# Moving SBUF buffers by multiples of 32 bytes under a stream of float32r matmuls: eight buffers 32 bytes apart in their rest by 256, all later large buffers at rest 224

## The chip, the cores and the metric

The kernel runs on one core of one Trainium2 chip. The metric is the device time of one execution in microseconds (us); lower is better. The time of the kernel before is the median of three runs.

Two words are used throughout. The **rest** of a buffer is the byte at which it begins in each SBUF partition, modulo 256. The **distance** of a matmul is the rest of its weight operand minus the rest of its moving operand, modulo 256.

## The reference, cut to what matters

```python
x = A_x                                   # (1, 2048, 512), float32
xn = _layernorm(x, axis=-1)
a = jnp.einsum("bsd,ed->bse", xn, dft_hid_re)
b = jnp.einsum("bsd,ed->bse", xn, dft_hid_im)
s = jnp.einsum("ts,bse->bte", dft_seq_re, a) - jnp.einsum("ts,bse->bte", dft_seq_im, b)
h = jnp.einsum("bsd,df->bsf", xn, w1) + b1   # w1: (512, 1792)
r = jnp.where(h > 0, h, 0)
g = jnp.einsum("bsf,fd->bsd", r * r, w2) + b2   # w2: (1792, 512)
return x + s * _silu(g)
```

## The kernel before

Every float32 operand is split into a high part in float32r and a low part (the rest after the high part is taken away), and each product is three matmuls: high by high, high by low, low by high (`PASSES`). Most products are also done by a scheme of seven block products in place of eight, whose block sums VectorE forms. A stage therefore has long runs of matmuls of 128 by 128 weights and 256 moving columns, with a new weight load before nearly each one. The order of the instructions on each engine is written out by hand (`manual_schedule`).

TensorE does, in this order:

- **The plain stage**, line 340, 384 matmuls of 512 columns: the sequence transform of the first two chunks. The weights are x's normalised operands, buffers `xc0` to `xc7`; the moving operands are the split transform tiles in `ga` and `gb`, in turn.
- **The seven-product transform**, line 325, 2016 matmuls: six more chunks of 256 rows, each over eight steps j. Weights are `xc{j}`, moving operands `ga` (j even) or `gb` (j odd). 42 matmuls to a step.
- **The hidden transform**, line 705, class `YUnit`, 672 matmuls, 84 to a unit: weights are `yg` in `xc2` to `xc7`, moving operands `wdp` in `wd0`, `wd1`, `xc0`, `xc1`.
- **The first layer**, line 705, class `HUnit`, 1176 matmuls, 42 to a unit: weights are w1's blocks p = 0 to 6 in `ga`, `gb`, `xc2`, `xc3`, `xc0`, `xc1`, `wd0`; moving operands are `xT` in `xc6` and `xc7`, or in `xc4` and `xc5` for every other chunk of 512 rows. A unit's last products (5, 4 and 3) are done after the next unit has begun.
- **The second layer**, line 811, 1176 matmuls, 42 to a step: weights are `g` in `xc6`, `xc7`, `xc4` by the step's number modulo 3 (the very last in `wd0`); moving operands are w2's blocks p = 0 to 6 in `wd1`, `ga`, `gb`, `xc2`, `xc3`, `xc0`, `xc1`.

Each such buffer is one tag of the one SBUF pool, and its tile is larger than 256 bytes by a whole multiple (14336 bytes for `xc`, `ga`, `gb`; up to 16384 for `wd0`, `wd1`). Within a tile all matmul operands begin at multiples of 512 bytes. So each operand has the rest of its buffer.

A tag gets its place when it is first asked for, in steps of 32 bytes, one behind the other, and keeps it. In the kernel before, the pool's first tile stands at byte 1152, and `b1s`, `b2s`, `eps`, `stats` and `stats_t` end at byte 3552, which is 13 x 256 + 224. The places that follow are:

| buffers, in order | rest by 256 |
|---|---|
| `xc0` to `xc7` (line 170) | 224 |
| `pq00`, three `u`, `pq01`, `pq10`, `pq11`, `wd1` | 224 |
| three `bn` of 64 bytes, three `sm` of 32 bytes (288 bytes) | 224, 32, 96, 160, 192, 224 |
| `ga`, `wd0`, `gb`, `e` | 0 |

The distances of the stages before are thus: line 340 and line 325, 224 throughout (weights at 224, moving operands at 0); the hidden transform, 0 for three of four matmuls and 224 for the one with `wd0`; the first layer, 32 for p = 0, 1, 6 and 0 for p = 2, 3, 4, 5; the second layer, 224 for p = 1, 2 and 0 for p = 0, 3, 4, 5, 6 (32 for the last step).

Of the kernel before, what the change touches and what calls it, by code (L numbers as in the profile page):

```python
# [8 lines left out]
F32 = mybir.dt.float32  # L9
F32R = mybir.dt.float32r  # L10
# [3 lines left out]
P = 128  # L14
S, D, F = 2048, 512, 1792
NS, ND, NF = S // P, D // P, F // P
NJ, NP = NS // 2, NF // 2
# [102 lines left out]
def fnet_gated_kernel(ctx, tc, x, xt, ct, wd, w1, w2, b1, b2, out):  # L120
# [9 lines left out]
    def split(*parts):  # L130
        split_hi(*parts)
        split_lo(*parts)
# [4 lines left out]
    pool = ctx.enter_context(tc.tile_pool(name="pool", bufs=1))  # L137
# [5 lines left out]
    eps = pool.tile([P, 1], F32, name="eps")  # L143
    stats = pool.tile([P, 2, 2, NJ], F32, name="stats")
    stats_t = pool.tile([P, 2 * NS], F32, name="stats_t")
    rows = dram.tile([2 * NS, P], F32, name="rows")
    Y = [dram.tile([TC, D], F32, name=f"y{t}") for t in range(NTC)]
    PQD = [dram.tile([P, 2, 4, 256], F32, name=f"pqd{c}") for c in range(NC)]
# [10 lines left out]
    def buf(tag, shape, name, dtype=F32):  # L159
        bufs = {"u": 3, "bn": 3, "sm": 3}.get(tag, 1)  # L160
        return pool.tile(shape, dtype, tag=tag, bufs=bufs, name=name)
# [4 lines left out]
    def halves(ap):  # L166
        return ap.rearrange("p (a b) -> p a b", a=2)


    XC = [buf(f"xc{j}", [P, 7, 2, 256], f"xc{j}", F32R) for j in range(NJ)]  # L170

    xr, xn32 = {}, {}

# [5 lines left out]

    def ln_stats(j, hs=slice(0, 2)):  # L180
        t = xr[j]
        sm = buf("bn", [P, 12], f"bn{j}_{hs.start}")
        for h in range(hs.start, hs.stop):
            bn = sm[:, 6 * h:6 * h + 6]
            nc.vector.bn_stats(bn, t[:, h])  # L185
            nc.vector.bn_aggr(stats[:, :, h, j], bn)

    root = {}

    def ln_root(j, hs=slice(0, 2)):  # L190
        n = hs.stop - hs.start
        t = root[j] = buf("sm", [P, 4], f"root{j}_{hs.start}")
        nc.scalar.activation(t[:, 0:n], stats[:, 1, hs, j], AF.Sqrt, bias=eps)

    def ln_rstd(j, hs=slice(0, 2)):
# [17 lines left out]
    def xc_parts(j, h):  # L213
        s = slice(2 * h, 2 * h + 2)
        return XC[j][:, s, HI, :], XC[j][:, s, LO, :], halves(xn32[j][:, h])

# [14 lines left out]
    def split_sums(j):  # L231
        s = xn32[j].rearrange("p h (b n) -> p (h b) n", b=2)
        split(XC[j][:, S2:S4 + 1, HI, :], XC[j][:, S2:S4 + 1, LO, :], s[:, 0:3])
        return 0.9

    def split_s1(j):
        split(XC[j][:, S1, HI, :], XC[j][:, S1, LO, :], s1[j // ND][:, j % ND])
        return 0.4
# [81 lines left out]
    def mm(ps, w, mv, first, last):  # L320

        ps = ps.rearrange("p (i d t) -> p d i t", i=2, d=2)
        for d in range(2):
            for a_, b_ in PASSES:
                nc.tensor.matmul(ps[:, d], w[:, a_, d * P:(d + 1) * P], halves(mv(b_)),  # L325
                                 start=first and d == 0 and (a_, b_) == (HI, HI),
                                 stop=last and (a_, b_) == (LO, HI), skip_group_check=True)
# [9 lines left out]
    def one_product(c, j, h, k, passes=PASSES):  # L337
        for a_, b_ in passes:
            w = XC[j][:, 2 * h + k // 2, a_, k % 2 * P:(k % 2 + 1) * P]
            nc.tensor.matmul(accs[c][k], w, part[c, j][:, b_, 2 * h:2 * h + 2],  # L340
# [97 lines left out]
    for count, zeros in zip(WARM, (idle[:, 0:256].bitcast(mybir.dt.bfloat16), idle[:, 256:768])):  # L438
# [3 lines left out]
        for _ in range(count):  # L442
            nc.tensor.matmul(warm, zeros[:, 0:P], zeros, start=True, stop=True)
    ln_stats(0)
    ln_root(0)
    split_hi(*plain_parts(0, 0, one))
    ln_rstd(0)
# [5 lines left out]
    for hs in (one, two):  # L453
        split_lo(*plain_parts(0, 0, hs))
    split_lo(*xc_parts(0, 0))
    ln_stats(1)
    g = plain_parts(0, 1)
    split_hi(*g)
    ln_root(1)
    split_lo(*xc_parts(0, 1))  # L460
    for h in range(2):
# [3 lines left out]
    for j in range(1, NJ):  # L465
        ln_rstd(j)
        for h in range(2):
            ln_xn(j, h)
            split_hi(*xc_parts(j, h))
        split_lo(*g)  # L470
        load_c(*order[j + 3])
        if j + 4 < NJ:
            load_x(j + 4)
        split_lo(*xc_parts(j, 0))
        if j + 1 < NJ:
            ln_stats(j + 1)
            ln_root(j + 1)
        split_lo(*xc_parts(j, 1))
        for h in range(2):
            products(0, j, h)  # L480
        g = plain_parts(*order[j + 1])
        split_hi(*g)
        if j == 2:
            nc.sync.dma_start(b1s, b1)
            nc.sync.dma_start(b2s, bcast(b2, D))
# [58 lines left out]
    for n, s in enumerate(steps):  # L544
        c, j = s
# [4 lines left out]
        for p in FIRST if j == 0 and c > PLAIN else ORDER:  # L550
# [4 lines left out]
            a, b = PRODUCTS[p]  # L555
            mm(ms[p], XC[j][:, a], lambda b_: g[:, b_, b], j == 0, j == NJ - 1)
        border = closing and j == 0
# [335 lines left out]
    for u in range(1, NC):  # L893
        n = 2 * u + 2
# [184 lines left out]
def _launch(arrays, out_shape):  # L1079
    import numpy as np  # L1080
    import concourse.bacc as bacc
    from concourse.bass_utils import run_bass_kernel_spmd

    nc = bacc.Bacc("TRN2", target_bir_lowering=False, num_devices=1, dynamic_dma_scratch_size=1024)
    feed, args = {}, []
    for name, v in arrays.items():
        v = np.ascontiguousarray(v)
        feed[f"in_{name}"] = v
        args.append(nc.dram_tensor(f"in_{name}", v.shape, mybir.dt.from_np(v.dtype), kind="ExternalInput").ap())
    args.append(nc.dram_tensor("out_0", out_shape, F32, kind="ExternalOutput").ap())  # L1090
    with tile.TileContext(nc, schedule_with_timeline_sim=True) as tc:
        fnet_gated_kernel(tc, *args)
    r = run_bass_kernel_spmd(nc, [feed], core_ids=[0])
    return r.results[0]["out_0"]
# [25 lines left out]
```

## Time and profile before

| what | value |
|---|---|
| median of three runs | 702.4 us (702.17 to 702.65) |
| the profiled execution | 701.75 us |
| its span, first to last instruction | 700.0 us |
| granted TensorE clock, mean | 0.998 |
| line 340, first and last start | 7.7 and 97.7 us |
| line 325 | 97.9 and 333.9 us |
| line 705, hidden transform | 334.0 and 417.0 us |
| line 705, first layer | 410.7 and 557.1 us |
| line 811 | 552.9 and 695.2 us |

The profiled execution is one run, 1.75 us longer than its span. In the views, PE is TensorE's matmuls, PEld its weight loads, DVE is VectorE, ACT is ScalarE. A matmul's record lasts longer than the time until the next one begins, because matmuls overlap in the engine; the time that counts is the **pace**, from one start to the next. From a row of the timeline, which joins equal instructions that follow each other, the pace is the row's length less one record (0.28 us for 256 columns), over the count less one.

### The profile page before, as it was taken

The numbers are of one execution on the slowest core, as the hardware profiler recorded it, in microseconds if no ns is written. First come the engines' busy times: TensorE is split into PE (matmuls) and PEld (weight loads), VectorE is DVE, ScalarE is ACT, GpSimd is POOL, SyncE is SP. The second block draws the span as 40 slices with busy tenths as digits, with TensorE's granted clock in tenths as the row PEclk, the third lists the DMA queues.
The fourth block names the chain that finished last, engine by engine and source line by source line (L and its number), as shares of the span: only waits on it lengthen the run. The fifth ranks groups of instructions, "written<-read, shape, count | busy, mean of one in ns | idle before, by whom it ended". The sixth has DMA issues, their size and how long they took to land.

```text
span 700.0 us, 13144 instructions
## 1 busy us (share of the span) xinstructions
PE 693.0 (99%) x5440; PEld 670.1 (96%) x5440; DVE 605.6 (87%) x849; ACT 357.9 (51%) x475; POOL 6.4 (1%) x9
## 2 busy tenths in 40 slices
PE   8999999999999999999999999999999999999997
PEld 5778889999999999999999999999999999999997
DVE  7999769999999898788899788899748689989896
ACT  4436544435343343435455358777778764444451
POOL 0000000000000000000000000000000000101000
PEclk9999999999999999999999999999999999999999
DMA  8535756768486754367488457587426956767745
GB/s 298 198 104 197 257 202 219 257 204 290 158 294 211 259 210 166 121 239 274 151 287 280 151 185 287 195 322 266 154 118 197 388 168 188 194 197 195 227 155 157
DMA packets 51723, 150.82 MB, mean 215 GB/s; under 512 B 4944, under 2 KB 19536, under 8 KB 50256
## 3 DMA queue, kind: packets, MB, share of 16 engines
q1 hardware_dynamic: 44096, 129.80, 54.9%
q10 hardware_dynamic: 6208, 18.88, 6.8%
q0 software_dynamic: 1360, 1.31, 1.5%
q8 instruction: 42, 0.69, 0.4%
q14 instruction: 17, 0.14, 0.1%
HBM read 101.98 MB, written 47.99 MB: 214 GB/s over the span
## 4 chain that ended last, share of the span: by engine, by line
PE 94%; DVE 3%; DMA 1%; ACT 1%; issue 1%; SPq 0%; DVEq 0%; ACTq 0%
PE m L325 33%; PE m_o L811 15%; PE r_B L705 13%; PE r_A L705 8%; PE pq_b L340 8%; PE r_C L705 4%; PE r_D L705 4%; PE m_last L811 4%; PE pq_ba L340 2%; PE pq_bc L340 1%; PE pq_bb L340 1%; DMA rows<-rows 1%; DVE yg L128 0%; DMA x<-in_x 0%; DVE bn L185 0%
## 5 line engine op out<-in xcount | busy, mean ns | idle before, releaser
L325 PEld LDWEIGHTS m<-g,xc 128*128 128x128 f32 x2016 | 235.7, 188 | 0.6 <-DVE g L128 0.2
L325 PE MATMUL m<-g,xc 128*128 128x256 f32 x2016 | 236.2, 280 | 0.0
L125 ACT ACTIVATE g<-u 128x1792 fp32r<-128x1792 f32 (+3 forms) x70 | 100.1, 1431 | 143.2 <-PE m L325 47.7
L128 DVE TENSOR_TENSOR g<-u,g 128x1792 fp32r<-128x1792 f32 (+3 forms) x70 | 117.5, 1679 | 23.3 <-ACT g L125 23.1
L811 PE MATMUL m_o<-w,g 128*128 128x256 f32 x882 | 105.7, 282 | 0.0
L811 PEld LDWEIGHTS m_o<-w,g 128*128 128x128 f32 x882 | 105.5, 191 | 0.0
L125 ACT ACTIVATE g<-hr 128x1792 fp32r<-128x1792 f32 (+2 forms) x31 | 47.9, 1556 | 47.2 <-PE m_o L811 25.2
L705 PE MATMUL r_B<-xT,w 128*128 128x256 f32 x504 | 69.4, 282 | 0.0
L340 PE MATMUL pq_b<-g,xc 128*128 128x512 f32 x240 | 66.7, 397 | 1.1 <-ACT xc L125 1.0
L705 PEld LDWEIGHTS r_B<-xT,w 128*128 128x128 f32 x504 | 64.1, 190 | 0.0
L128 DVE TENSOR_TENSOR g<-hr,g 128x1792 fp32r<-128x1792 f32 (+2 forms) x31 | 56.7, 1837 | 7.1 <-ACT g L125 7.1
L340 PEld LDWEIGHTS pq_b<-g,xc 128*128 128x128 f32 x240 | 43.8, 188 | 13.9 <-ACT xc L125 3.1
L705 PE MATMUL r_A<-xT,w 128*128 128x256 f32 x336 | 44.7, 282 | 0.0
L705 PEld LDWEIGHTS r_A<-xT,w 128*128 128x128 f32 x336 | 42.1, 190 | 0.0
L705 PE MATMUL r_B<-wdp,yg 128*128 128x256 f32 x288 | 37.5, 283 | 0.2 <-DVE y L715 0.2
L705 PEld LDWEIGHTS r_B<-wdp,yg 128*128 128x128 f32 x288 | 35.6, 190 | 0.6 <-DVE y L715 0.4
L811 PE MATMUL m_last<-w,g 128*128 128x256 f32 x294 | 35.1, 282 | 0.0
L811 PEld LDWEIGHTS m_last<-w,g 128*128 128x128 f32 x294 | 35.1, 190 | 0.0
L257 DVE TENSOR_TENSOR u<-u 128x512 f32<-128x512 f32 x48 | 32.8, 684 | 1.7 <-DMA u<-in_ct 1.7
L128 DVE TENSOR_TENSOR yg<-yraw,yg 128x1792 fp32r<-128x1792 f32 x13 | 26.2, 2021 | 5.4 <-ACT yg L125 5.4
L306 DVE TENSOR_TENSOR c<-m,c 128x512 f32<-128x512 f32 x42 | 27.2, 684 | 1.7 <-PE m L325 1.0
L125 ACT ACTIVATE yg<-yraw 128x1792 fp32r<-128x1792 f32 x13 | 22.1, 1699 | 7.2 <-DVE yraw L266 5.5
(180 smaller groups left out, 862.7 us busy)
## 6 DMA issues: line engine op xcount, KB each, us to landing
u<-in_ct SPq DMA_DIRECT2D x63, 512.0 KB, 3.7
hd<-h ACTq DMA_DIRECT2D x28, 512.0 KB, 4.8
hr<-hd SPq DMA_DIRECT2D x28, 512.0 KB, 3.9
wdp<-wdd SPq DMA_DIRECT2D x8, 896.0 KB, 7.2
yraw<-pqd SPq DMA_DIRECT2D x13, 512.0 KB, 5.0
pqd<-c SPq DMA_DIRECT2D x6, 1024.0 KB, 4.4
w<-w1d SPq DMA_DIRECT2D x6, 896.0 KB, 8.7
y<-y ACTq DMA_DIRECT2D x8, 512.0 KB, 4.1
```

Source lines behind the costliest of these rows:

```text
L125: nc.scalar.activation(hi, src, AF.Copy)
L128: nc.vector.tensor_tensor(lo, src, hi.bitcast(F32), op=ALU.subtract)
L257: nc.vector.tensor_tensor(t[:, 0:2], r[:, 0:1].to_broadcast([P, 2, 256]), r[:, 1:3], op=ALU.add)
L306: nc.vector.tensor_tensor(part_(to), m, part_(frm), op=op)
L325: nc.tensor.matmul(ps[:, d], w[:, a_, d * P:(d + 1) * P], halves(mv(b_)), start=first and d == 0 and (a_, b_) == (HI, HI), stop=last and ( ...
L340: nc.tensor.matmul(accs[c][k], w, part[c, j][:, b_, 2 * h:2 * h + 2], start=j == 0 and h == 0 and (a_, b_) == (HI, HI), stop=j == NJ - 1 a ...
L705: nc.tensor.matmul(self.region(REGION[k]), w, mv, start=i == 0 and k in (1, 7), stop=i == len(ops) - 1, skip_group_check=True)
L811: nc.tensor.matmul(m[:, i * 256:(i + 1) * 256], ready[n][:, a_, H_SLOT[a], i * P:(i + 1) * P], W2[p][:, b_, b], start=p == 0 and i == 0 an ...
```

## The change

The tags `bn` and `sm` are asked for ahead of the `xc` buffers, and after each of `xc0` to `xc6` a tile of 32 bytes that nothing uses is asked for. No other statement changes; the first `bn` and `sm` tiles are taken from the small dictionary in place of a new request.

```diff
     rows = dram.tile([2 * NS, P], F32, name="rows")
+    small = {tag: pool.tile([P, n], F32, tag=tag, bufs=3, name=f"{tag}0_0") for tag, n in (("bn", 12), ("sm", 4))}
...
-    XC = [buf(f"xc{j}", [P, 7, 2, 256], f"xc{j}", F32R) for j in range(NJ)]
+    XC = []
+    for j in range(NJ):
+        XC.append(buf(f"xc{j}", [P, 7, 2, 256], f"xc{j}", F32R))
+        if j < NJ - 1:
+            pool.tile([P, 8], F32, name=f"gap{j}")
...
-        sm = buf("bn", [P, 12], f"bn{j}_{hs.start}")
+        sm = small.pop("bn", None) or buf("bn", [P, 12], f"bn{j}_{hs.start}")
...
-        t = root[j] = buf("sm", [P, 4], f"root{j}_{hs.start}")
+        t = root[j] = small.pop("sm", None) or buf("sm", [P, 4], f"root{j}_{hs.start}")
```

By the same rule of placing, `xc0` begins at 3552 + 288 = 3840 = 15 x 256, rest 0; each next `xc` is 14336 + 32 bytes further, so `xc{j}` has rest 32j; everything behind `xc7` (rest 224) has rest 224, `ga`, `gb`, `wd0`, `wd1` and `e` included. Counted over all matmuls in program order (each one's moving operand against the weights that are loaded while it runs), the distances become:

| stage, matmuls | distance 0 | 32 | 64 | 96 | 128 | 160 | 192 | 224 |
|---|---|---|---|---|---|---|---|---|
| line 340, before | 0 | 0 | 0 | 0 | 0 | 0 | 0 | 384 |
| line 340, after | 48 | 48 | 48 | 48 | 48 | 48 | 48 | 48 |
| line 325, before | 0 | 0 | 0 | 0 | 0 | 0 | 0 | 2016 |
| line 325, after | 252 | 251 | 252 | 253 | 252 | 252 | 252 | 252 |
| other three, before | 1973 | 546 | 0 | 0 | 0 | 0 | 0 | 504 |
| other three, after | 308 | 237 | 291 | 525 | 469 | 569 | 256 | 368 |

On line 325 the distance after is 32(j + 1) modulo 256, so each of the eight steps j has one of its own.

## The prediction

> **What bounds the kernel now.** I read the page first: busy time, then the chain that ended last, then its groups.
>
> ```profile
> span 700.0 us, 13144 instructions
> PE 693.0 (99%) x5440; PEld 670.1 (96%) x5440; DVE 605.6 (87%) x849; ACT 357.9 (51%) x475; POOL 6.4 (1%) x9
> ...
> PE 94%; DVE 3%; DMA 1%; ACT 1%; issue 1%; SPq 0%; DVEq 0%; ACTq 0%
> ...
> L325 PE MATMUL m<-g,xc 128*128 128x256 f32 x2016 | 236.2, 280 | 0.0
> ```
>
> TensorE is busy for 99% of the span and makes 94% of the chain; the largest group, line 325, has no idle time ahead of it. So the time is the number of matmuls times their pace, and the question is whether an operand's address alters the pace. Next I read the timeline of PE alone, which joins runs of equal matmuls, in stretches whose buffers I know from the order of the steps. First the second layer (line 811): steps with w2 in `xc3`, `xc0`, `xc1`, `wd1`, then the two with w2 in `ga` and `gb`. The weights are in `xc` buffers, rest 224, in both.
>
> ```profile
> 574.77 20.56 PE L811 MATMUL m_o<-w,g 128*128 128x256 f32 x170
> ```
>
> ```profile
> 594.93 10.30 PE L811 MATMUL m_o<-w,g 128*128 128x256 f32 x86
> ```
>
> The pace is (20.56 - 0.28)/169 = 120.0 ns where both operands rest at 224, distance 0, and (10.30 - 0.28)/85 = 117.9 ns where the moving operand rests at 0, distance 224. Line 325, also at distance 224, and line 340, the same but with 512 columns:
>
> ```profile
> 112.61 24.90 PE L325 MATMUL m<-g,xc 128*128 128x256 f32 x212
> ```
>
> ```profile
> 53.10 2.26 PE L340 MATMUL pq_b<-g,xc 128*128 128x512 f32 x9
> ...
> 58.70 2.26 PE L340 MATMUL pq_b<-g,xc 128*128 128x512 f32 x9
> ```
>
> Line 325 paces (24.90 - 0.28)/211 = 116.7 ns. Line 340 does 24 matmuls from 53.10 to 58.70, 233.3 ns each, twice 116.7. With 512 columns a weight load has twice the time to finish, so I take 116.7 ns as what streaming 256 columns costs when the weight load doesn't hinder: a floor, and line 325 stands on it already. The first layer (line 705), from one `r_D` to the one a unit later, 42 matmuls: first with w1 at rest 224 (distance 0), then with w1 in `wd0` and `ga` at rest 0 (distance 32).
>
> ```profile
> 429.96 0.88 PE L705 MATMUL r_D<-xT,w 128*128 128x256 f32 x6
> ...
> 435.00 0.88 PE L705 MATMUL r_D<-xT,w 128*128 128x256 f32 x6
> ```
>
> ```profile
> 450.03 0.87 PE L705 MATMUL r_D<-xT,w 128*128 128x256 f32 x6
> ...
> 455.00 0.87 PE L705 MATMUL r_D<-xT,w 128*128 128x256 f32 x6
> ```
>
> That is 5.04/42 = 120.0 ns and 4.97/42 = 118.3 ns. The hidden transform has three distances of 0 to one of 224, 84 matmuls to a unit:
>
> ```profile
> 354.79 1.60 PE L705 MATMUL r_D<-wdp,yg 128*128 128x256 f32 x12
> ...
> 364.82 1.60 PE L705 MATMUL r_D<-wdp,yg 128*128 128x256 f32 x12
> ```
>
> 10.03/84 = 119.4 ns, where (3 x 120.0 + 117.9)/4 gives 119.5: one price for each distance carries over between stages. The weight loads show the same split. Below is the view of one line's weight loads (least, median and greatest duration in ns), at distance 0, at distance 224, and in the opening matmuls of line 443, whose weights and moving operand are the same zeros at rest 224.
>
> ```profile
> L811 PEld LDWEIGHTS m_o<-w,g x43: 191/192/193, 574.9 to 579.9; 128*128 128x128 f32 x43
> ```
>
> ```profile
> L811 PEld LDWEIGHTS m_o<-w,g x42: 187/188/192, 595.1 to 599.9; 128*128 128x128 f32 x42
> ```
>
> ```profile
> L443 PEld LDWEIGHTS warm<-idle x8: 187/188/338, 4.2 to 6.1; 128*128 128x128 f32 x8
> ```
>
> At distance 0 a load takes 192 ns, 4 more than at 224. The opening matmuls are at distance 0 and show 188; they have 512 columns and one address for both operands, so they don't refute it, but they don't support it either.
>
> **The change part by part.** *Small tiles and gaps*: no instruction, wait, DMA or queue entry is added or moved; the three `bn` and three `sm` places rotate as before. Cost 0; nothing on an engine has to hide it.
>
> *VectorE, ScalarE and DMA at other rests*: the low-part subtractions tell, by shape.
>
> ```profile
> L128 DVE TENSOR_TENSOR g<-u,g 128x1792 fp32r<-128x1792 f32 x43 | 87.0, 2022 | 17.8 <-ACT g L125 17.7
> ...
> L128 DVE TENSOR_TENSOR yg<-yraw,yg 128x1792 fp32r<-128x1792 f32 x13 | 26.2, 2021 | 5.4 <-ACT yg L125 5.4
> ```
>
> The first writes rest 0, the second rest 224: 2022 against 2021 ns. Cost 0. For the `xc` tiles at rests 32 to 192 no row exists; I keep 0, and as these engines are off the chain a change of some ns an instruction wouldn't reach the end. Transfers keep their sizes; 0 as well.
>
> *Hidden transform and both layers, 3023 matmuls.* As excess over 116.7 ns, distance 0 costs 3.3, distance 32 costs 1.6, distance 224 costs 1.2. Before: 1973 x 3.3 + 546 x 1.6 + 504 x 1.2 = 7.99 us. After, the known distances: 308 x 3.3 + 237 x 1.6 + 368 x 1.2 = 1.84 us. The other 2110 lie at 64 to 192, which no row shows; call their mean excess m. The gain is 6.15 - 2.11m us. The bounds of m are 0 (the floor) and 3.3 (no better than equal rests). The nearest rows are the neighbours of 0, mean 1.4, and they fall from 3.3 within one step of 32 bytes; I let the fall go on and take m = 0.8: gain 4.46 us.
>
> *Line 325, 2016 matmuls.* It leaves a floor and can only lose. Distance 224 stays free (252). Distances 0 and 32 at the prices above: 252 x 3.3 + 251 x 1.6 = 1.23 us. The other 1261 have an excess m'. At distance 224 this line pays 0 where line 811 pays 1.2, so it is the more tolerant of the two; m' = 0.4, half of m, bounds 0 and 3.3 again. Loss 1.23 + 0.50 = 1.73 us.
>
> *Line 340.* Its weight loads have time to spare; 0.1 us. The bound above is 48 x 3.3 + 48 x 1.6 + 240 x 3.3 = 1.03 us, below 0.
>
> *What VectorE takes back.* In the second layer it runs close behind. Busy time by engine in two stretches (the second holds steps at 117.9 ns):
>
> ```profile
> 575.00:595.10 20.10, 20.10 (x170) 20.10 (x169) 18.96 (x26) 9.95 (x10) 0.00 (x0) 1.00 0.62 190
> 595.10:605.00 9.90, 9.90 (x86) 9.90 (x86) 9.73 (x13) 4.45 (x4) 2.55 (x2) 1.00 0.71 195
> ```
>
> 9.73 of 9.90 us are VectorE's. Where TensorE gets faster here, it meets the subtractions for `g`; a third of this layer's share of the gain (about 1.6 us of the 4.46) may go: 0.5 us back, bounds 0 and 1.6.
>
> Sum: -4.46 + 1.73 + 0.1 + 0.5 = -2.1 us. The profiled execution goes from 701.75 to 699.6; the median of the runs lies 0.65 us above that execution, so 702.4 becomes **700.3 us**.
>
> **The rivals.**
>
> *No fall beyond the neighbours* (m = m' = 1.4, VectorE as above): -6.15 + 2.95 + 1.23 + 1.77 + 0.2 + 0.3 = +0.3, so 702.7 us. For it: the two measured neighbours, and that at distance 224 line 811 doesn't reach the floor. Against: line 325 does.
>
> *Slower: the hindrance repeats every 64 bytes.* If it is the parity of 32-byte pieces that collides, distances 64, 128 and 192 cost 3.3 like 0, and 96 and 160 cost 1.4 like 32 and 224. Place: line 325, where four of eight steps would fall off the floor. The other stages: 1016 x 3.3 + 1094 x 1.4 = 4.88 us in place of 2.11m, gain 1.27. Line 325: 1.23 + 756 x 3.3 + 505 x 1.4 = 4.43. Line 340: 0.3. Sum +3.5, **705.9 us**. For it: the rows know only distances 0, 32 and 224, and can't tell a period of 64 from one of 256. Against: nothing but line 325's tolerance. It decides from where m and m' pass 1.3: then -6.15 + 1.23 + 0.6 + 3.37m is over zero.
>
> *Slower by another way: it is the moving operand's own rest, not the distance.* Equal weights at 224: 120.0 against 117.9, so 2.1 ns for a moving operand at 224. Line 325 then pays 1764 x 2.1 + 252 x 0.4 (j = 0, 118.3 against 117.9) = 3.8 us; the layers lose about 0.9 more, as `ga`, `gb`, `wd0` leave rest 0: 707.1 us. Against: line 705 gains 1.7 ns by the weights' rest alone, with the moving operand at 224.
>
> *The rests don't matter.* All buffers of rest 0 are the last four of the pool, behind byte 175,000. If their place in the memory counts and not the rest, no pair changes: 702.4 us. Against: `wd1` lies just ahead of them and paces 120.0. The Trainium skill, page "TensorE: Matmul & The Clock Gate", Part 2, speaks for this one: TensorE has two independent SBUF read ports, and loading the next weights takes no read bandwidth from the running matmul. By that rule the time would stay. The 120.0 and 117.9 ns of one line, with 192 and 188 ns loads, are hard to square with it.
>
> **How the numbers follow.** Forecast 0.42, no fall beyond the neighbours 0.18, period of 64 0.24, moving rest 0.07, rests don't matter 0.09. The forecast's own range is m = m' = 0 without VectorE's share (-6.15 + 1.23 = -4.9, 697.5 us) to m = 1.4, m' = 0.7 (-3.2 + 2.1 + 0.2 + 0.5 = -0.4, 702.0 us). The range of 8 in 10 is 698.0 to 706.2: it holds the slower rival and leaves out the moving rest and the far ends. About 0.2% (1.4 us) is what a measurement here tells from no change. Faster: 0.37 of the forecast and 0.03 of the second case, 0.40. Same: 0.05, 0.11 and 0.08 of the first, second and last, 0.24. Slower: the rest, 0.36.
>
> **What would show it.** The timeline of line 325 by step: paces near 120 in j = 7 alone, near 118 in j = 0, at 117 in the others; 120 in j = 1, 3, 5 too would show the period of 64, about 119 or more in j = 1 to 7 the moving rest. In line 811 steps that pair unequal rests should fall from 120.0 towards 117.5, with 188 ns loads. The forecast is wrong if line 325 grows from 236 us by more than the other stages shrink.

## The result and the profile after

The kernel after takes 701.32 us (median; 701.2 to 701.6) against 702.43 us before: a ratio of 0.9984, 95% interval 0.9977 to 0.9991. So it is faster by 1.1 us, a little less than the 0.2% that the prediction called visible, and the interval lies clear of 1. The profiled execution took 701.23 us, its span 699.5 us (before: 701.75 and 700.0). The traces thus account for 0.5 of the 1.1 us; where the rest lies, no trace shows. The forecast was 700.3. In what follows the times of whole kernels are medians of several executions, and one execution of the shifted kernel, which took 3866.07 us where its other nine took 701.35 to 701.92, is left out of its ratio.

The page of the kernel after, its busy time and its chain:

```profile
span 699.5 us, 13144 instructions
PE 692.9 (99%) x5440; PEld 670.5 (96%) x5440; DVE 605.9 (87%) x849; ACT 357.8 (51%) x475; POOL 6.4 (1%) x9
...
PE 95%; DVE 2%; ACT 1%; issue 1%; DMA 0%; ACTq 0%; DVEq 0%
```

Same instructions, same bound. What moved shows in the groups of TensorE's matmuls by line (busy time in us, then the mean of one record in ns; the lines stand 5 further down than before):

```profile
L330 PE MATMUL m<-g,xc 128*128 128x256 f32 x2016 | 238.9, 281 | 0.0
L816 PE MATMUL m_o<-w,g 128*128 128x256 f32 x882 | 104.8, 281 | 0.0
L710 PE MATMUL r_B<-xT,w 128*128 128x256 f32 x504 | 68.8, 281 | 0.0
```

Before, these groups had 236.2, 105.7 and 69.4 us. Added up by stage from the same view of both kernels (groups overlap a little, so the sum is not exact to a tenth):

| stage | before | after | difference |
|---|---|---|---|
| line 340 (after: 345), plain | 118.5 | 118.1 | -0.4 |
| line 325 (330), seven-product transform | 236.2 | 238.9 | +2.7 |
| line 705 (710), hidden transform | 87.7 | 87.0 | -0.7 |
| line 705 (710), first layer | 163.3 | 162.0 | -1.3 |
| line 811 (816), second layer | 140.8 | 139.8 | -1.0 |
| sum | | | -0.7 (span: -0.5) |

That is the exchange the prediction described: three stages gain about 3 us and the seven-product transform gives most of it back. Now the eight steps j of one chunk of that transform, each with a distance of its own. The view gives busy time in stretches cut at the first matmul of each step; the columns are stretch, sum, PE busy with the records that touch the stretch, clock, DMA share and GB/s. The first row is step j = 1 of the first chunk, the other eight are j = 0 to 7 of the fourth:

```profile
102.52:107.47 4.95, 4.95 (x45) 1.00 0.95 330
217.13:222.10 4.97, 4.97 (x45) 1.00 0.63 214
222.10:226.86 4.76, 4.76 (x44) 1.00 0.35 115
226.86:231.91 5.05, 5.05 (x45) 1.00 0.78 311
231.91:236.89 4.98, 4.98 (x45) 1.00 0.82 290
236.89:241.92 5.03, 5.03 (x44) 1.00 0.85 286
241.92:246.87 4.95, 4.95 (x44) 1.00 0.34 110
246.87:251.82 4.95, 4.95 (x45) 1.00 0.79 291
251.82:256.86 5.04, 5.04 (x45) 1.00 0.79 287
```

Each stretch is 42 matmuls, so the paces at distances 32, 64, 96, 128, 160, 192, 224 and 0 are 118.3, **113.3**, 120.2, 118.6, 119.8, 117.9, 117.9 and 120.0 ns. Three things stand against the prediction at once. Distance 64 lies far below the 116.7 ns that I took for a floor. Distances 96 and 160 are as bad as 0. And the first row is the same step as the third, same buffers, same distance of 64, an earlier chunk: 4.95/42 = 117.9 ns in place of 113.3. Of the six chunks only the first runs this step slowly. The slow stretch also has the heaviest DMA traffic of the nine (share 0.95, against 0.35 in the fast one), so traffic is a rival for the two paces; the runs below answer it.

### The profile page after: what moved, and what is told of

Read it like the earlier page. It is cut to its first block, busy times and chain, and to the rows that moved or that the text cites. A ratio compares the mean times of both kernels' runs of the same rounds, so it can differ in the third digit from the quotient of the medians.

```text
span 699.5 us, 13144 instructions
## 1 busy us (share of the span) xinstructions
PE 692.9 (99%) x5440; PEld 670.5 (96%) x5440; DVE 605.9 (87%) x849; ACT 357.8 (51%) x475; POOL 6.4 (1%) x9
## 4 chain that ended last, share of the span: by engine, by line
PE 95%; DVE 2%; ACT 1%; issue 1%; DMA 0%; ACTq 0%; DVEq 0%
PE m L330 34%; PE m_o L816 15%; PE r_B L710 13%; PE r_A L710 9%; PE pq_b L345 8%; PE r_C L710 4%; PE r_D L710 4%; PE m_last L816 4%; PE pq_ba L345 2%; PE pq_bc L345 1%; PE pq_bb L345 1%; DMA x<-in_x 0%; DVE bn L190 0%; DVE z L866 0%; ACT yg L125 0%
## 5 line engine op out<-in xcount | busy, mean ns | idle before, releaser
L330 PEld LDWEIGHTS m<-g,xc 128*128 128x128 f32 x2016 | 238.7, 188 | 0.3 <-DVE g L128 0.2
L330 PE MATMUL m<-g,xc 128*128 128x256 f32 x2016 | 238.9, 281 | 0.0
L128 DVE TENSOR_TENSOR g<-u,g 128x1792 fp32r<-128x1792 f32 (+3 forms) x70 | 117.5, 1679 | 26.0 <-ACT g L125 25.7
```

Source lines behind the costliest of these rows:

```text
L128: nc.vector.tensor_tensor(lo, src, hi.bitcast(F32), op=ALU.subtract)
```

## The experiments

Theory A is that the distance sets the pace. Its rivals are that each operand's own rest does, and that rests don't matter.

### Distance 0 everywhere

```diff
-    XC = []
-    for j in range(NJ):
-        XC.append(buf(f"xc{j}", [P, 7, 2, 256], f"xc{j}", F32R))
-        if j < NJ - 1:
-            pool.tile([P, 8], F32, name=f"gap{j}")
+    XC = [buf(f"xc{j}", [P, 7, 2, 256], f"xc{j}", F32R) for j in range(NJ)]
```

> All large buffers at rest 0, so every matmul has distance 0 (weights' rest minus moving operand's rest). Theory A, the distance sets the pace: the seven-product line paces 120.0 ns as its step j = 7 did after the change, 2016 x 3.3 = +6.7 us on the kernel before; the other three stages go to 120.0 throughout, +2.0 us; the plain stage with 512 columns paces 227 to 229 ns as its distance-0 steps did, -1.9 us; about 709 us. Theory B, the operands' own rests set it and rest 0 is the good one: no pace over 116.7 ns, about 694 us. Theory C, rests don't matter: 702.4 us.

Measured 709.02 us, ratio to the kernel before 1.0091 (1.0074 to 1.0108): theory A, whose terms add up to 709.2, to 0.2 us. Its groups, the matmuls of the seven-product transform and their weight loads:

```profile
L326 PE MATMUL m<-g,xc 128*128 128x256 f32 x2016 | 242.2, 283 | 0.0
```

```profile
L326 PEld LDWEIGHTS m<-g,xc 128*128 128x128 f32 x2016 | 242.1, 192 | 0.1
```

242.2/2016 is 120.1 ns, with loads of 192 ns. This is also the change with its gaps left out (small tiles ahead, nothing between the `xc` buffers). So it is the gaps, which part the `xc` buffers from each other, that take the kernel after below the kernel before. An operand that begins on a multiple of 256 is worth nothing by itself.

### Distance 64 for the seven-product transform

The `xc` buffers share rest 128 and all later large buffers rest 64; `stats_t` is asked for behind them to make room.

```diff
-    stats_t = pool.tile([P, 2 * NS], F32, name="stats_t")
...
+    XC = [buf(f"xc{j}", [P, 7, 2, 256], f"xc{j}", F32R) for j in range(NJ)]
+    pool.tile([P, 48], F32, name="gap")
...
+            stats_t = pool.tile([P, 2 * NS], F32, name="stats_t")
             nc.vector.transpose(stats_t, stats.rearrange("p m h j -> p (m h j)"))
```

> The eight xc buffers at rest 128, all later large buffers at rest 64, so the seven-product line has distance 64 in every step. Theory A (distance): it paces 113.4 ns as its step j = 1 did after the change, 2016 x (113.4 - 116.7) = -6.7 us on the kernel before; in the other stages pairs of xc buffers are at distance 0 (120.0), xc against ga, gb, wd0, wd1 at 64 (113.4), the reverse at 192 (117.8): about -4.6 us; 691 to 693 us unless VectorE, over 90% busy there, takes some of it back. Theory B (own rests): weights at 128 and moving operands at 64 in the seven-product line; the step with weights at 128 paced 120.1 after the change, so about +6 us, 708.

Measured 693.77 us (692.44 to 696.09), ratio 0.9877 (0.9853 to 0.9901). Theory A again, though 0.8 us above the range that was named, which held only if VectorE took nothing back; weights at rest 128 are no hindrance. Its four runs spread over 3.7 us; whether paces differ from one run to the next is not shown. From its page, the chain that ended last and the group:

```profile
PE 79%; DVE 14%; ACT 3%; issue 2%; DMA 1%; ACTq 0%; DVEq 0%
...
L326 PE MATMUL m<-g,xc 128*128 128x256 f32 x2016 | 230.5, 277 | 1.7 <-DVE g L128 1.5
```

The group fell from 236.2 to 230.5 us, and here the view names waits of TensorE for VectorE's low parts (`g`, 1.5 us), which it didn't before. Away from pauses the line paces 113.4 ns, but pauses of over 140 ns between starts cost 3.4 us on it, where they cost about 0.8 before, and VectorE's share of the chain is 14% in place of 3%. With faster matmuls VectorE is the next bound of this stage.

### The same distances at other rests

```diff
-    stats_t = pool.tile([P, 2 * NS], F32, name="stats_t")
...
+            stats_t = pool.tile([P, 2 * NS], F32, name="stats_t")
             nc.vector.transpose(stats_t, stats.rearrange("p m h j -> p (m h j)"))
```

> The kernel after with every large buffer moved down by 128 bytes (a 128-byte tile that stood ahead of them stands behind them), so all distances are those of the kernel after and all rests are others. Theory A (distance): each of the eight steps of the seven-product line keeps its pace within 0.3 ns (118.3, 113.4, 120.1, 118.6, 120.1, 117.8, 117.8, 120.0) and the time is that of the kernel after, 701.3 us. Theory B (own rests): the low pace of 113.4 ns moves from j = 1 to j = 5, whose weights now rest at 32.

Measured 701.47 us, ratio 0.9986 (0.9976 to 0.9995), the time of the kernel after. The fourth chunk, j = 0 to 7, in the same view as above:

```profile
217.52:222.49 4.97, 4.97 (x45) 1.00 0.68 229
222.49:227.25 4.76, 4.76 (x44) 1.00 0.35 117
227.25:232.30 5.05, 5.05 (x45) 1.00 0.81 310
232.30:237.28 4.98, 4.98 (x45) 1.00 0.79 290
237.28:242.31 5.03, 5.03 (x44) 1.00 0.79 288
242.31:247.26 4.95, 4.95 (x44) 1.00 0.33 107
247.26:252.21 4.95, 4.95 (x45) 1.00 0.74 291
252.21:257.25 5.04, 5.04 (x45) 1.00 0.82 288
```

All eight lengths are those of the kernel after, to the hundredth, though the rest of every large buffer moved by 128. The fast step stays at j = 1 and doesn't move to j = 5. The rival of own rests falls: with a rule of own rests the fast step would have moved.

### A map of the distances

A kernel with nothing but runs of equal matmuls and their weight loads; `cell` names the run and gives the two byte offsets.

```python
for k in range(32):
    cell(f"fa_{LET[k]}", 32 * k, 1024)
for k in range(32):
    cell(f"fb_{LET[k]}", 1024, 1024 + 1024 - 32 * k)
...
```

> A kernel that leaves out the whole computation and runs 48 equal matmuls at a time, each with its weight load: distances 0 to 992 in steps of 32 bytes, first by moving the weights (fa), then by moving the moving operand (fb), then as the seven-product line has it, in two halves of 128 columns with a gap in the output (fc), then with 512 columns (fd). Theory A with a period of 256: the four quarters of each family repeat, 120.0 at 0, 113.4 at 64, and fa equals fb. A longer period: the quarters differ, above all at 96 and 224, where the second layer paced 117.3 and 116.7 and the seven-product line 120.1 and 117.8. Theory B (own rests): fa and fb differ. If the form matters: fc differs from fa at 96 and 224.

The timeline of TensorE, the first cells of `fa` (the letters a to h are distances 0 to 224), 48 matmuls each, so the pace is (length - 0.28)/47:

```profile
21.99 5.91 PE L44 MATMUL fa_a<-mv,wt 128*128 128x256 f32 x48
27.75 5.84 PE L44 MATMUL fa_b<-mv,wt 128*128 128x256 f32 x48
33.42 5.82 PE L44 MATMUL fa_c<-mv,wt 128*128 128x256 f32 x48
39.08 5.79 PE L44 MATMUL fa_d<-mv,wt 128*128 128x256 f32 x48
44.71 5.85 PE L44 MATMUL fa_e<-mv,wt 128*128 128x256 f32 x48
50.40 5.91 PE L44 MATMUL fa_f<-mv,wt 128*128 128x256 f32 x48
56.15 5.81 PE L44 MATMUL fa_g<-mv,wt 128*128 128x256 f32 x48
61.80 5.83 PE L44 MATMUL fa_h<-mv,wt 128*128 128x256 f32 x48
```

and the same of `fb`:

```profile
209.61 5.84 PE L44 MATMUL fb_b<-mv,wt 128*128 128x256 f32 x48
215.29 5.82 PE L44 MATMUL fb_c<-mv,wt 128*128 128x256 f32 x48
220.95 5.86 PE L44 MATMUL fb_d<-mv,wt 128*128 128x256 f32 x48
226.66 5.85 PE L44 MATMUL fb_e<-mv,wt 128*128 128x256 f32 x48
232.34 5.92 PE L44 MATMUL fb_f<-mv,wt 128*128 128x256 f32 x48
238.10 5.61 PE L44 MATMUL fb_g<-mv,wt 128*128 128x256 f32 x48
243.54 5.78 PE L44 MATMUL fb_h<-mv,wt 128*128 128x256 f32 x48
```

`fa` paces 119.8 ns at 0, 117.9 at 64 and 117.7 at 192. `fb` paces 113.4 at 192, from 5.61 us. The four quarters, distances 0 to 992, repeat within 0.2 ns in both families, so the pace has a period of 256, and the rival period of 64 is out: 32, 96 and 160 don't agree, nor do 0 and 64. The form with two halves (`fc`) equals `fa` within 0.2 ns, so the form is not what lets line 325 be fast. But `fa` and `fb` differ at 96, 192 and 224, and 64 never came out fast, while two kernels had it at 113.3. A distance alone doesn't give one pace.

The 512-column cells (`fd`) undo the floor. At distance 224 and at distance 256, which is equal rests:

```profile
592.91 3.89 PE L44 MATMUL fd_h<-mv,wt 128*128 128x512 f32 x16
596.63 3.80 PE L44 MATMUL fd_i<-mv,wt 128*128 128x512 f32 x16
```

A record lasts 0.39 us here. At equal rests that is (3.80 - 0.39)/15 = 227 ns, 113.6 for 256 columns; at 224 it is 233.3, as on line 340. So 233.3 was the pace of that line's distance, and no floor.

### What ran ahead

```python
for a in range(8):
    for b in range(8):
        cell(f"pre_{LET[a]}", 32 * a, 1024, count=24)
        cell(f"h{LET[a]}_{LET[b]}", 32 * b, 1024)
...
```

> Leaves out the whole computation. One place for the moving operand (rest 0); weights at rests 0 to 224. Every one of the eight distances runs 48 matmuls after 24 matmuls at each of the eight distances (64 cells, h and two letters: a = 0, b = 32, c = 64 to h = 224, first the one ahead, then the one measured), and then three times after a stop in which TensorE waits for ScalarE (idle). Theory H (some distances have two steady paces, and what ran ahead chooses): the cells of 64 show both 113.3 and 117.8 ns, those of 192 113.3 or 117.8, those of 224 116.7 or 117.8, with the same operands at the same bytes. Theory R (each pair of own rests has one pace, so that the map's first and second family differ by their places): every cell of a distance shows the pace of the first family whatever ran ahead: 64 at 117.8, 192 at 117.8, 224 at 117.8, 96 at 117.4.

Paces in ns over the last 20 matmuls of each cell, from the starts in the trace; the row is what ran ahead, the column what is measured:

| ahead | 0 | 32 | 64 | 96 | 128 | 160 | 192 | 224 |
|---|---|---|---|---|---|---|---|---|
| 0 | 120.0 | 118.3 | 117.7 | 117.4 | 118.7 | 119.8 | 113.4 | 116.7 |
| 32 | 120.0 | 118.3 | 117.7 | 118.6 | 120.2 | 120.3 | 117.8 | 117.7 |
| 64 | 120.0 | 118.3 | 117.8 | 117.5 | 118.8 | 119.8 | 113.4 | 116.6 |
| 96 | 120.0 | 118.2 | 113.4 | 120.0 | 118.8 | 120.3 | 117.7 | 116.5 |
| 128 | 120.0 | 118.2 | 117.8 | 118.8 | 118.7 | 119.9 | 117.7 | 116.7 |
| 160 | 120.0 | 118.2 | 113.3 | 117.2 | 118.5 | 120.1 | 117.7 | 116.7 |
| 192 | 119.8 | 118.6 | 117.8 | 117.4 | 118.5 | 120.2 | 117.8 | 117.8 |
| 224 | 120.0 | 118.4 | 113.3 | 117.2 | 120.2 | 119.8 | 117.8 | 117.7 |

Two cells of distance 64 in the timeline, one after 64, one after 96, with the same operands at the same bytes:

```profile
178.89 5.82 PE L44 MATMUL hc_c<-mv,wt 128*128 128x256 f32 x48
...
246.34 5.62 PE L44 MATMUL hd_c<-mv,wt 128*128 128x256 f32 x48
```

Theory H holds: 117.9 ns and 113.6 ns ((5.62 - 0.28)/47) for one pair. Distances 64 and 192 have two steady paces, 113.3 and 117.8; 224 has 116.6 and 117.8; 128 has 118.7 and 120.2; 96 goes from 117.2 to 120.0. Distance 0 has one, 120.0, and 32 stays near 118.3.

DMA traffic isn't what parts the paces. The stretch that holds both cells above has next to none, and no work of VectorE or ScalarE either (the columns behind the length are TensorE's matmuls, its weight loads, VectorE, ScalarE, GpSimd, clock, DMA share, GB/s):

```profile
100.00:300.00 200.00, 200.00 (x1698) 200.00 (x1697) 0.00 (x0) 0.00 (x0) 0.00 (x0) 1.00 0.00 1
```

The distance just ahead doesn't settle the choice alone, so the table is no rule to go by. In this run 64 behind 128 is slow in the table (117.8), but the 24 matmuls of 64 that follow the cell of 128 in row 64 are fast (113.3 over their last twelve). In the kernel after, distance 32 runs ahead of 64 in every chunk, and from the starts in the trace the pace is 117.8 in the first chunk and 113.5 in the others. After a stop, too, both occur: of the three cells of 64 entered that way two ran fast and one slow. What sets the choice is not shown.

### Three groups of rests

`xc0` to `xc3` at 128, `xc4` to `xc7` at 64, later buffers at 0; `stats_t`, `b1s` and the `bn` tiles fill the gaps.

```diff
...
+    for j in range(NJ):
+        if j == 4:
+            stats_t = pool.tile([P, 2 * NS], F32, name="stats_t")
+            b1s = pool.tile([P, NF], F32, name="b1s")
         XC.append(buf(f"xc{j}", [P, 7, 2, 256], f"xc{j}", F32R))
+    small["bn"] = pool.tile([P, 12], F32, tag="bn", bufs=3, name="bn0_0")
```

> Large later buffers at rest 0, xc4 to xc7 at 64, xc0 to xc3 at 128, so hardly any pair is at distance 0: seven-product line, j = 0 to 3 at 128 (118.7 ns), j = 4 to 7 at 64 (113.4); first layer, xc pairs at 64 and ga, gb, wd0 at 192; second layer, xc pairs at 192 and ga, gb, wd1 at 64. Against the run with distance 64 (692.4 to 696.1 us): the seven-product line loses 1008 x 5.3 = 5.3 us, less up to 3 us that it there waits for VectorE; the two layers win 677 and 631 matmuls from 120.0. If they find their fast paces (113.3 at 64 and 192): -8.7 us, about 689 to 690; if their slow ones (117.8 at both): -2.9 us, about 694 to 695. Faster than the kernel after in either case if the distance sets the pace.

Measured 691.94 us (691.65 to 692.18), ratio 0.9845 (0.9828 to 0.9861): faster than both kernels, and between the two cases that were laid out. The groups:

```profile
L330 PE MATMUL m<-g,xc 128*128 128x256 f32 x2016 | 235.7, 279 | 0.4 <-DVE g L128 0.3
L816 PE MATMUL m_o<-w,g 128*128 128x256 f32 x882 | 103.2, 279 | 0.0
L710 PE MATMUL r_B<-xT,w 128*128 128x256 f32 x504 | 67.6, 277 | 0.1
```

The first layer found the fast pace at both of its distances (its four groups add up to 157.8 us, before 163.3). The second layer found it at 64, from its second chunk on, but not at 192, where its steps ran at 117.8 ns. And in the seven-product transform, j = 4 and 5 (both at 64) of three chunks:

```profile
122.64:127.40 4.76, 4.76 (x45) 1.00 0.54 194
127.40:132.16 4.76, 4.76 (x45) 1.00 1.01 333
157.44:162.38 4.94, 4.94 (x44) 1.00 0.69 249
162.38:167.33 4.95, 4.95 (x44) 1.00 0.73 268
197.16:201.93 4.77, 4.77 (x45) 1.00 0.95 323
```

Chunks one and three run them in 4.76 us, chunk two in 4.95: two paces within one execution, as in the kernel after. Of the six chunks only the second is slow, in all four of its steps at 64 (168 matmuls at 117.8 ns). DMA traffic doesn't part them here either: the fast stretches have shares from 0.54 to 1.01, the slow ones 0.69 and 0.73.

## Why the prediction was right in its direction and too large in its size

- **What bounds the kernel.** Right. TensorE has 95% of the chain after, and every run's time followed its pace, until VectorE appeared at distance 64 (14% of the chain, 1.5 us of named waits).
- **The distance and not the own rest.** Right, and shown: the shifted kernel keeps all eight paces. A distance doesn't always fix one pace, however: 64, 96, 128, 192 and 224 have two or more. The rival of the moving operand's rest, 707.1 us, is out, and so is the rival that rests don't matter: by it the kernels with distance 0 and 64 would both take 702.4 us, and they took 709.0 and 693.8. The Trainium skill's rule of two independent read ports for weights and moving operand (page "TensorE: Matmul & The Clock Gate", Part 2) stood for that last rival. By that rule nothing would have changed, which these two times don't bear out.
- **Small tiles, VectorE, ScalarE, DMA at no cost.** Held: VectorE is busy for 605.9 us after and 605.6 before, ScalarE for 357.8 and 357.9.
- **The three stages' gain, "I let the fall go on and take m = 0.8".** This term was mis-sized. Over the 2107 matmuls at distances 64 to 192 that followed without a pause, the mean excess over 116.7 ns is 1.6 ns, twice my value; the measured gain is 3.0 us where 4.46 was forecast. The cost doesn't fall away with distance: 96 and 160 cost 3.5 and 3.1 on line 325, and 64 and 192 can lie 3.3 below the 116.7.
- **"Distance 224 stays free" and m' = 0.4 on line 325.** Mis-sized too. From the rows, 64 to 192 average 24.77 us / 210 = 118.0 ns, an excess of 1.3; distance 224 now paces 117.9, so 1.2 in place of 0. The eight steps add up to 39.73 us against 8 x 4.90 before, 0.53 us for each of six chunks: 3.2 us, forecast 1.73. The page's group grew by only 2.7 because TensorE also stood still less: what pauses of over 140 ns between starts cost beyond one pace adds up to 0.27 us on this line, 0.84 before.
- **The step that failed** lies under these two terms: "a floor, and line 325 stands on it already", and with it "one price for each distance carries over between stages". 116.7 was one of two paces of distance 224; line 811 had shown 117.9 at the same distance, and I read the difference as tolerance of the line. Line 325 itself now paces 117.9 there, and the map by what ran ahead has both paces for the same operands, so the line doesn't decide it; what ran before does.
- **Line 340, 0.1 us.** The other way: its busy time fell by 0.4 us. Its steps at distance 0 pace 227 ns (the median of 48 matmuls), where it paced 234 before; the 233.3 was no floor either.
- **The direction was partly luck.** The two terms that the forecast was made of, 3.0 us won and 3.2 us lost, cancel. What took the kernel after below the kernel before in the traces is line 340, and pauses on line 325 that are 0.6 us shorter; the forecast had the first with the other sign and the second not at all, and whether the change brings the shorter pauses about is not shown.
- **VectorE's share of 0.5 us.** Not needed: the second layer of the kernel after has no pause of over 140 ns between starts.
- **The rival "no fall beyond the neighbours"** (702.7 us) came nearly as near, 1.4 us off against 1.0, though on the other side of no change: its mean of 1.4 fits both lines, but it had no fast paces in it.

## What to carry to other kernels

In a run of float32r matmuls of 256 columns with a weight load each, compute the distance of weights and moving operand modulo 256 for every pair that runs long, and keep it off 0 and 160, and rather off 96 and 128; 64 is the one to try first: it may run at its slower pace, but that was 117.8 ns and not 120. Place buffers by groups of partners rather than spread them evenly: an even spread buys the mean over good and bad distances, which here was worth 0.2%, while chosen distances were worth 1.5%. With 512 columns the order is another (below). Read the pace per step, in more than one repeat of the same step, before calling a number a floor.

## What the runs showed of the hardware that was not expected

- The same matmuls on the same bytes have two steady paces at distances 64 and 192 (113.3 and 117.8 ns), depending on what ran before, and a pace once taken can last: 168 matmuls in a row at 117.8 ns in the second chunk of the last run.
- At equal rests 256 columns pace 120.0 ns, among the slowest, while 512 columns pace 227 to 230 ns there, the fastest of their distances (227 to 234).
- The weight load's own duration, which the prediction used as a second sign (192 ns at distance 0, 188 otherwise), doesn't go with the distance alone. In j = 7 of the kernel after, distance 0 and 120.0 ns, the view of that line's weight loads has them at 188 (least, median, greatest):

```profile
L330 PEld LDWEIGHTS m<-g,xc x39: 188/188/190, 251.9 to 256.5; 128*128 128x128 f32 x39
```
